# A new order for the opening of an attention-plus-MLP kernel, more staging places for its weight blocks, and more low halves on GpSimd

## The chip, the cores and the metric

One NeuronCore of a Trainium2 chip runs the kernel. The metric is the device time of one execution in microseconds (us). PE is TensorE, DVE is VectorE, ACT is ScalarE, POOL is GpSimd, and SP is the queue that issues most DMAs.

## The reference

```
a    = softmax(phi)                      # b,h,s,m   b=8 h=8 s=576 m=32
k_m, v_m = a^T k, a^T v                  # b,h,m,d   d=64
attn = softmax(q k_m^T / 8)              # b,h,s,m
x    = concat over heads of attn @ v_m   # 4608 tokens x 512
h    = x @ w_in                          # 512 -> 2048
out  = (h - tanh(h)) @ w_out             # 2048 -> 512
```

Inputs are float32, the weights come as 64-bit floats, and the output is 4608 x 512 float32.

## The kernel before

The weights are not applied to x. Per batch b the kernel folds v_m into w_in: P(b, fb) = v_m @ w_in for each of four blocks fb of 512 hidden columns. A unit u is 256 tokens (18 units, and some lie across two batches), so h(u, fb) = attn @ P(b, fb). A polynomial for h - tanh(h) follows, and then the product with w_out. To get nearly float32 accuracy out of 16-bit matmuls, each factor is split into a high and a low half (f16), and three products of halves are summed.

The work is written by hand as a list of words, and at the end every engine's instructions are pinned to the order in which they were written (`in_order`). So each engine, and each DMA queue, is a strict queue: an instruction that waits holds up all that stand behind it. The list `START` is the opening. It covers units 0 to 3 and the first two blocks of unit 4; after it a loop (steady part) runs the same steps for the other 54 blocks by a plan. The words:

- `iK:tag` and `oK:tag` load one 512 KB block K of w_in or w_out (as 64-bit words) into a buffer of the ring `tag`; with the tags `kv2` and `kv3` two blocks. In the profile these are the tiles `raw` and `raws` (L373, L380). A ring with n buffers can take a new load only when the (n)th load before it has been consumed; until then SP waits, and all later loads with it.
- `FX` and `FA` load phi in two layouts (tiles `pt` and `e`), `KA` and `KB` load k and v (tile `kv`, and `kt`), and `Q` loads q for one half t of a batch (tile `q`, L139).
- `Tpp` converts a pair p of weight blocks to float32 on DVE (L386, L391, L396, two instructions each, into `wt`, by way of the ring in `W_TAG`) and casts the high half on ACT (L408). Its low half is made by `Lp` (PE and ACT), by `Lv` (DVE, L421, two instructions) or by `L` (a scaling on ACT, L437, and a subtraction on POOL, L440, two each). Pairs 0 to 7 are w_in (two pairs for one fb), 8 to 15 w_out.
- `X`, `YX`, `XT`, `V`, `N`, `U`, `UV`: softmax of phi, k_m and v_m, the transpose to `kT`, `vh` and `vl`. `S` forms scores (psc, L278); `AM`, `AE`, `AD`, `AT`, `AS` are the softmax over them and its split into `ah` and `al`. `AM` and `AD` subtract and multiply on POOL (L308, L321), and `AS` makes `al` on POOL, `ASv` on DVE (both L522).
- `P` and `PL` (or `PLp`) make the halves of P. `Hufb` is the first matmul (L579). The words `a` and `ap` run the polynomial: DVE L594, ACT L599, DVE L604, ACT L610 (the high half of g). With `ap` the first DVE step leaves its result in PSUM; with `a` it goes to one of two `h3` buffers in SBUF. The low half of g is made by `c` on POOL or by `cv` on DVE (both L615). `Mufb` is the second matmul (24 matmuls, L658); its last eight need the low half.
- `Z` is two matmuls of no use to the result, which fill gaps on PE (tile `warm`, L798). `G`, `R`, `OP`, `O` prepare the steady part and store results.

Of the kernel before, what the change touches and what calls it, by code (L numbers as in the profile page):

```python
# [63 lines left out]
START = """
i0:gg i1:gg T00 T00 Z00 Z00 FX0 T00 X0 T00 YX0 Z00 Z00 Z00 Z00 Z00 Z00 Z00 Z00 Z00 Z00 i6:kv3 T03 i4:kv2 T03 i2:gg Z00
T02 T03 i3:gg T02 T02 Z00 KA0 Z00 Z00 Z00 KB0 Lp00 Lp00 o2:gg o3:gg Q00 T01 T03 XT0 Lp03 XT0 V00 Z00 Z00 T01 T01 T02
Q01 T01 o4:gg Lv01 o5:pp2 V01 N0 Z00 U0 L02 U0 Z00 S00 Z00 S01 T09 T09 T09 S00 o6:gg KA1 L02 KB1 AM00 S01 AM00 Lp03 UV0
UV0 o7:gg AM01 W0 T09 AM01 AE00 AE01 AD00 AD01 AD00 AT00 AD01 Z00 Z00 Z00 P00 AT01 FX1 P00 Lp09 PLp00 Z00 ASv00 P01
PLp00 ASv00 T10 Lp09 P01 AS01 H00 H00 T10 T11 PL01 i10:kv3 o9:pp4 X1 Q10 ap00 Q11 o1:gg AS01 T10 o0:pp2 T11 YX1 ap00
H10 XT1 T11 ap00 H10 XT1 T10 Lv10 ap00 c00 V10 V11 T11 L11 H11 N1 a10 U1 T08 i8:kv2 T08 UV1 U1 S10 UV1 T08 KA2 a10 T08  # L70
H11 a10 S10 H01 Lv08 a10 c10 S11 M00 ap11 AM10 W1 P10 H01 o10:pp5 o8:gg ap11 S11 ap11 M10 AM10 AE10 AM11 KB2 FA2 P10
Q20 AD10 L11 AM11 ap01 PL10 Q21 P11 T12 T12 ap01 AE11 ap11 AD10 T12 cv11 T12 P11 M11 AT10 AD11 AS10 AS10 ap01 H20 PL11
AD11 Lv12 AT11 T05 T05 ap01 T05 H21 OP1 cv01 H20 FX2 T05 ap20 H21 AS11 ap20 o11:gg AS11 X2 ap20 M01 a21 H31 L05 OP0 T04
T04 T04 a21 ap20 cv20 XP2 a21 H31 ap31 Y2 T04 L05 i14:kv3 L04 a21 L04 H30 c21 H30 a30 T13 M20 Y2 P02 i12:kv2 M21 T13
ap31 a30 P02 T13 V20 V21 a30 PL02 ap31 H02 H12 T06 T06 T06 T13 L13 OP2 T06 P12 a30 Lv06 ap31 T07 T07 N2 T07 cv30 T07 W2
M30 Lv07 P12 o12:kv2 cv31 H02 PL12 a02 P03 H12 P03 a02 T14 T14 T14 PL03 M31 ap12 a02 FA3 T14 OP3 L13 U2 ap12 Lv14 U2
UV2 o14:kv3 UV2 a02 H13 S20 ap12 S20 H13 ap12 H03 c02 AM20 a13 H03 T15 a03 P13 M02 P13 a13 S21 PL13 c12 AM20 H22 T15
a03 H23 a13 AE20 a13 G00 c13 S21 P20 AMv21 H22 AD20 a22 T15 T15 AD20 a03 a03 a22 G01 Lv15 AT20 P20 H23 a22 AMv21 AE21
cv03 ap23 R1 a22 ASv20 PL20 M12 ap23 M13 P21 ap23 FQ3 H32 ap23 P21 H32 ASv20 O1 O1 AD21 PL21 a32 H40 H40 G10 ap40 c22
R0 AD21 cv23 G20 AT21 ap40 a32 G11 ap40 H41 M03 H33 P22 AS21 H33 a32 a32 M22 P22 c32 O0 M23 X3 G21 H41 ap41 G30 ap33  # L80
G31 PL22 ap41 O0 ap33 ap40 KR30 R2 P23 P23 O2 ap41 c40 AS21 O2 ap33 ap33 F40 cv33 ap41 M32 M33 R3 O3 O3 PL23 c41
"""
# [261 lines left out]
def split_path(ctx, tc, c, ins, out):  # L344
# [37 lines left out]
    def to_f32(p, ts):  # L382

        r32 = [raws.pop(2 * p + i).bitcast(U32).rearrange("p (f w) -> p f w", w=2) for i in range(2)]
        for r, t in zip(r32, ts):
            nc.vector.tensor_scalar(  # L386
                t, r[:, :, 1], 3, 0x3FFFFFFF, op0=ALU.logical_shift_left, op1=ALU.bitwise_and
            )
        yield
        for r, t in zip(r32, ts):  # L390
            nc.vector.scalar_tensor_tensor(  # L391
                t, r[:, :, 0], 29, t, op0=ALU.logical_shift_right, op1=ALU.bitwise_or
            )
# [708 lines left out]
@with_exitstack  # L1102
def tile_kernel(ctx: ExitStack, tc: tile.TileContext, qt, kva, kvt, pha, phx, w_in, w_out, out):
    nc = tc.nc
    ins = dict(qt=qt, kva=kva, kvt=kvt, pha=pha, phx=phx, w_in=w_in, w_out=w_out)
# [8 lines left out]
    nc.vector.tensor_scalar(c["nid16"], c["ident"], -1.0, None, op0=ALU.mult)
# [50 lines left out]
```

## Time and profile before

| | |
|---|---|
| median of 3 runs | 655.64 us (655.16 to 656.02) |
| profiled execution, its own time | 652.95 us |
| span of the profiled execution | 651.2 us |
| mean granted TensorE clock | 0.999 |
| PE busy | 631.0 us, 97% |
| DVE busy | 525.5 us, 81% |
| ACT busy | 375.0 us, 58% |
| POOL busy | 250.8 us, 39% |
| end of the opening (first matmul of tile `hs`) | 191.91 us |

The time of an execution is 1.75 us more than its span, and the profiled one was 2.69 us below the median of the timed runs. The profile's rows are in us from the span's start; a step of an engine begins when the step before it on that engine has begun to drain, so the distance between two starts is some 0.08 us shorter than a duration on DVE, and for matmuls much shorter.

### The profile page before, as it was taken

The numbers are of one execution on the slowest core, as the hardware profiler recorded it, in microseconds if no ns is written. First come the engines' busy times: TensorE is split into PE (matmuls) and PEld (weight loads), VectorE is DVE, ScalarE is ACT, GpSimd is POOL, SyncE is SP. The second block draws the span as 40 slices with busy tenths as digits, with TensorE's granted clock in tenths as the row PEclk, the third lists the DMA queues.
The fourth block names the chain that finished last, engine by engine and source line by source line (L and its number), as shares of the span: only waits on it lengthen the run. The fifth ranks groups of instructions, "written<-read, shape, count | busy, mean of one in ns | idle before, by whom it ended". The sixth has DMA issues, their size and how long they took to land.

```text
span 651.2 us, 15451 instructions
## 1 busy us (share of the span) xinstructions
PE 631.0 (97%) x6618; PEld 451.7 (69%) x6618; DVE 525.5 (81%) x786; ACT 375.0 (58%) x505; POOL 250.8 (39%) x173
## 2 busy tenths in 40 slices
PE   8679999999999999999999999999999999999996
PEld 4255656566557768777777777777787777887885
DVE  6889999999956687877888879787979786867773
ACT  4477686666524456544655565545655677666541
POOL 0225141222132254452536353635452455455531
PEclk9999999999999999999999999999999999999999
DMA  8999344301422302145313522441354333234201
GB/s 342 390 381 372 109 179 168 119 15 67 147 97 104 135 33 73 37 153 171 104 49 143 170 65 75 155 145 60 106 156 135 102 115 113 67 113 133 79 33 38
DMA packets 27724, 85.51 MB, mean 131 GB/s; under 512 B 3584, under 2 KB 4096, under 8 KB 26880
## 3 DMA queue, kind: packets, MB, share of 16 engines
q1 hardware_dynamic: 26352, 82.08, 36.8%
q10 hardware_dynamic: 1296, 2.36, 1.0%
q8 instruction: 54, 0.88, 0.6%
q14 instruction: 22, 0.18, 0.1%
HBM read 72.89 MB, written 11.54 MB: 130 GB/s over the span
## 4 chain that ended last, share of the span: by engine, by line
PE 68%; DVE 21%; ACT 4%; issue 3%; DMA 2%; POOL 1%; DVEq 0%; ACTq 0%; POOLq 0%
PE hs L579 17%; PE x L722 12%; PE o L715 11%; PE o L722 8%; PE o L658 6%; DVE f L628 4%; PE h L579 4%; PE o1h L658 3%; DVE h L604 3%; DVE h L594 3%; DMA raw<-in_w_out_dram 2%; PE pp L531 2%; DVE ph L549 2%; DVE wt L391 1%; PE warm L798 1%
## 5 line engine op out<-in xcount | busy, mean ns | idle before, releaser
L615 POOL TENSOR_TENSOR g<-h,g 128x1024 f16<-128x1024 f32 x64 | 138.0, 2157 | 323.7 <-ACT g L610 223.8
L579 PEld LDWEIGHTS <-ph 128*128 128x128 f16 x2304 | 177.4, 98 | 19.5 <-issue 5.6
L579 PE MATMUL hs<-ah,ph 128*128 128x256 f16 (+3 forms) x1152 | 151.4, 246 | 0.0
L594 DVE SCALAR_TENSOR_TENSOR h<-hs,u 128x1024 f32<-128x1024 f32 x54 | 65.9, 1221 | 81.2 <-ACT u L586 81.2
L610 ACT ACTIVATE g<-h 128x1024 f16<-128x1024 f32 x72 | 76.0, 1057 | 94.5 <-DVE h L604 92.5
L579 PE MATMUL hs<-al,ph 128*128 128x256 f16 (+3 forms) x576 | 127.6, 246 | 0.0
L599 ACT ACTIVATE u<-u,beta 128x1024 f32<-128x1024 f32 x72 | 82.5, 1149 | 55.4 <-DVE h L594 54.4
L715 PE MATMUL o<-wout_hi,g 128*128 128x512 f16 x432 | 104.7, 379 | 0.0
L722 PEld LDWEIGHTS <-f 128*128 128x128 f16 x896 | 87.7, 98 | 10.2
L604 DVE SCALAR_TENSOR_TENSOR h<-u,h 128x1024 f32<-128x1024 f32 x72 | 87.4, 1216 | 0.8 <-ACT u L599 0.7
L722 PE MATMUL x<-bt,f 128*128 128x256 f16 x672 | 82.5, 273 | 0.0
L722 PEld LDWEIGHTS <-g 128*128 128x128 f16 x672 | 64.4, 98 | 25.8 <-issue 3.8
L586 ACT ACTIVATE u<-hs 128x1024 f32<-128x1024 f32 x54 | 55.1, 1020 | 44.4 <-PE hs L579 39.5
L628 DVE TENSOR_TENSOR f<-g 128x512 f16<-128x512 f16 x112 | 68.6, 652 | 4.3 <-POOL g L615 3.4
L715 PEld LDWEIGHTS <-g 128*128 128x128 f16 x432 | 40.6, 98 | 43.8 <-issue 8.0
L658 PEld LDWEIGHTS <-g 128*128 128x128 f16 x384 | 36.7, 98 | 46.5 <-issue 3.4
L658 PE MATMUL o<-wout_hi,g 128*128 128x512 f16 x192 | 58.8, 379 | 0.0
L579 PE MATMUL h<-ah,ph 128*128 128x256 f16 (+3 forms) x384 | 49.6, 246 | 0.4 <-DVE h L604 0.4
L579 PE MATMUL h<-al,ph 128*128 128x256 f16 (+2 forms) x192 | 42.4, 246 | 0.2 <-POOL al L522 0.2
L549 DVE SCALAR_TENSOR_TENSOR ph<-pp,ph 128x1024 f16<-128x1024 f32 x31 | 37.6, 1214 | 1.4 <-ACT ph L544 1.4
L544 ACT ACTIVATE ph<-pp 128x1024 f16<-128x1024 f32 x32 | 32.6, 1018 | 7.5 <-PE pp L531 5.1
L658 PE MATMUL o<-wout_lo,g 128*128 128x512 f16 x96 | 36.4, 379 | 0.0
(145 smaller groups left out, 962.3 us busy)
## 6 DMA issues: line engine op xcount, KB each, us to landing
q<-in_qt_dram SPq DMA_DIRECT2D x16, 576.0 KB, 4.4
...
```

The source lines that it names most:

```text
L549: nc.vector.scalar_tensor_tensor(pl, pa, S_P / (S_V * S_W), ph, op0=ALU.mult, op1=ALU.subtract)
L579: nc.tensor.matmul(hp[:, k, tu : tu + w], px[:, g, cs], d[ax][:, g, ta : ta + w], start=(n == 0), stop=(n == 5),)
L586: nc.scalar.activation(uu, hp, AF.Square, scale=1.0 / (S_A * S_P))
L594: nc.vector.scalar_tensor_tensor(h3, hp, C2 * S_G / (S_A * S_P), uu, op0=ALU.mult, op1=ALU.mult)
L599: nc.scalar.activation(uu, uu, AF.Square, bias=c["beta"])
L604: nc.vector.scalar_tensor_tensor(h3, uu, CC, hp, op0=ALU.add, op1=ALU.mult)
L610: nc.scalar.activation(gg[:, 0], h3, AF.Copy)
L615: eng.tensor_tensor(gg[:, 1], h3, gg[:, 0], op=ALU.subtract)
L628: nc.vector.tensor_tensor(o, x, y, op=op)
L658: nc.tensor.matmul(o, gx[:, k, P * tt : P * tt + P], wx[:, 4 * fb + k, :], start=(first and k == 0 and wx is wout_hi and gx is gh), stop=( ...
L715: nc.tensor.matmul(o[th], gg[:, 0, k, P * th : P * th + P], wout_hi[:, 4 * fb + k, :], start=(first and k == 0), stop=False)
L722: nc.tensor.matmul(dst, a(1 - n, kk), b(n, kk), start=(new and kk == 0 and n == 0), stop=(end and kk == 1 and n == 1))
```

## The change

Three things in one edit. The list `START` is written anew: the same steps in another order, with other rings for the loads. `W_TAG` spreads the float32 weights over four rings instead of two: two new ones, `us` and `qt`, which hold a pair in one place and are otherwise used by the steady part. And other variants of the same step are chosen: of the 16 low halves of weight pairs 10 instead of 5 are made on POOL, 5 instead of 8 on DVE, 1 instead of 3 on PE and ACT; of the 18 low halves of g 16 instead of 10 on POOL; `al` always on POOL; one multiplication `AD` on DVE; and 14 instead of 8 of the 18 polynomials run by `a` instead of `ap`. The steady part is untouched.

```diff
 START = """
-i0:gg i1:gg T00 T00 Z00 Z00 FX0 T00 X0 T00 YX0 Z00 Z00 Z00 Z00 Z00 Z00 Z00 Z00 Z00 Z00 i6:kv3 T03 i4:kv2 T03 i2:gg Z00
...
+Z00 Z00 KB0 Z00 Z00 FX0 i3:pp4 Z00 i2:h3 Z00 Z00 X0 Z00 Z00 KA0 T01 YX0 XT0 T01 i0:sc Z00 i1:pp1 T01 Q00 XT0 V00 V01
...
-W_TAG = ["pr" if p in (1, 3, 9, 11) else "ot" for p in range(16)]
+W_TAG = "pr us us qt qt ot us pr pr ot us us ot qt qt us".split()
...
+    def new_pair(p):
+        if W_TAG[p] in ("us", "qt"):
+            t = big.tile([P, 2, 512], U32, tag=W_TAG[p], name=f"wt{p}", bufs=1)
+            return [t[:, i] for i in range(2)]
+        return [big.tile([P, 512], U32, tag=W_TAG[p], name=f"wt{p}{i}") for i in range(2)]
+
     def conv(p):
 
-        ts = [big.tile([P, 512], U32, tag=W_TAG[p], name=f"wt{p}{i}") for i in range(2)]
+        ts = new_pair(p)
         yield from to_f32(p, ts)
```

Lines behind the new function stand six further down in the changed kernel (L440 becomes L446, L615 becomes L621).

First place: the SP queue up to the loads of q for batch 0. The number behind `raw` is the block (0 to 15 w_in, 16 to 31 w_out), `kv00` and `kv01` are the two halves of k and v. Before, from the eighth load on:

```order
L373 DMA raw2_158<-in_w_in_dram 128x512
L373 DMA raw3_168<-in_w_in_dram 128x512
L113 DMA kv00_176<-in_kva_dram 128x2064
L121 DMA kt0_178<-in_kvt_dram 128x516
L113 DMA kv01_186<-in_kva_dram 128x2064
L373 DMA raw18_194<-in_w_out_dram 128x512
L373 DMA raw19_196<-in_w_out_dram 128x512
L139 DMA q00_198<-in_qt_dram 128x1152
L139 DMA q01_253<-in_qt_dram 128x1152
```

After, from the first load:

```order
L113 DMA kv01_106<-in_kva_dram 128x2064
L104 DMA pt0_112<-in_phx_dram 128x1152
L373 DMA raw3_114<-in_w_in_dram 128x512
L373 DMA raw2_118<-in_w_in_dram 128x512
L113 DMA kv00_130<-in_kva_dram 128x2064
L121 DMA kt0_132<-in_kvt_dram 128x516
L373 DMA raw0_153<-in_w_in_dram 128x512
L373 DMA raw1_157<-in_w_in_dram 128x512
L139 DMA q00_161<-in_qt_dram 128x1152
L139 DMA q01_207<-in_qt_dram 128x1152
```

The two loads of q were the 15th and 16th of the queue, behind ten weight blocks that shared the three buffers of `gg` and the two of each `kv` pair; they are now the 9th and 10th, behind four weight blocks that lie in four different places.

Second place: POOL, from the first low half of g. Before:

```order
L615 TENSOR_TENSOR g00_592<-h300_581,g00_592 128x1024
L615 TENSOR_TENSOR g10_740<-h310_670,g10_740 128x1024
L308 TENSOR_TENSOR sc1_698<-sc1_698,sm10_779 128x576
L440 TENSOR_TENSOR wout_lo_100<-wt110_513,wout_hi_99 128x512
L440 TENSOR_TENSOR wout_lo_100<-wt111_514,wout_hi_99 128x512
L308 TENSOR_TENSOR sc1_698<-sc1_698,sm11_847 128x576
L321 TENSOR_TENSOR sc1_698<-sc1_698,sz10_857 128x576
L522 TENSOR_TENSOR al1_942<-af1_935,ah1_941 128x2x288
L321 TENSOR_TENSOR sc1_698<-sc1_698,sz11_937 128x576
L522 TENSOR_TENSOR al1_942<-af1_935,ah1_941 128x2x288
```

After:

```order
L446 TENSOR_TENSOR wout_lo_100<-wt90_510,wout_hi_99 128x512
L446 TENSOR_TENSOR wout_lo_100<-wt91_511,wout_hi_99 128x512
L446 TENSOR_TENSOR wout_lo_100<-wt80_519,wout_hi_99 128x512
L446 TENSOR_TENSOR wout_lo_100<-wt81_520,wout_hi_99 128x512
L308 TENSOR_TENSOR sc1_682<-sc1_682,sm10_697 128x576
L621 TENSOR_TENSOR g00_695<-h300_515,g00_695 128x1024
L621 TENSOR_TENSOR g10_703<-h310_622,g10_703 128x1024
L321 TENSOR_TENSOR sc1_682<-sc1_682,sz10_739 128x576
L446 TENSOR_TENSOR wout_lo_100<-wt10_700,wout_hi_99 128x512 x2
L308 TENSOR_TENSOR sc1_682<-sc1_682,sm11_808 128x576
L528 TENSOR_TENSOR al1_838<-af1_835,ah1_837 128x2x288
L621 TENSOR_TENSOR g11_806<-h311_737,g11_806 128x1024
```

Four low halves of w_out now stand ahead of the first low half of g on this queue, and the low halves of g(1,1) and later blocks have come onto it.

Third place: DVE around `dg2`, for which PE waits with the first matmul of batch 2 (tile `pmx`). Before:

```order
L396 SCALAR_TENSOR_TENSOR wt51_1002<-raws10_518,wt51_1002 128x512
L615 TENSOR_TENSOR g01_1007<-h301_945,g01_1007 128x1024
L594 SCALAR_TENSOR_TENSOR h20_947<-h20_947,u20_1069 128x1024
L151 TENSOR_REDUCE mx2_1083<-pt2_1071 128x2
L157 TENSOR_TENSOR dg2_1085<-ident_58,mx2_1083 128x256
L604 SCALAR_TENSOR_TENSOR h320_1087<-u20_1069,h20_947 128x1024
```

After:

```order
L391 SCALAR_TENSOR_TENSOR wt4_1013<-raws8_565,wt4_1013 128x512 x2
L610 SCALAR_TENSOR_TENSOR h320_949<-u20_941,h320_949 128x1024
L396 SCALAR_TENSOR_TENSOR wt4_1013<-raws8_565,wt4_1013 128x512 x2
L151 TENSOR_REDUCE mx2_1084<-pt2_883 128x2
L157 TENSOR_TENSOR dg2_1086<-ident_58,mx2_1084 128x256
L386 TENSOR_SCALAR wt70_1100<-raws14_1016 128x512
```

The low half of g(0,1) has gone from this queue to POOL, and the whole conversion of pair 4 and the second polynomial step of g(2,0) now stand ahead of `dg2`.

More of the change, by code (lines that the diff above doesn't have):

```diff
@@ L64 @@
 START = """
-i0:gg i1:gg T00 T00 Z00 Z00 FX0 T00 X0 T00 YX0 Z00 Z00 Z00 Z00 Z00 Z00 Z00 Z00 Z00 Z00 i6:kv3 T03 i4:kv2 T03 i2:gg Z00
[L66 to L79, printed above, removed]
@@ L80 @@
-R0 AD21 cv23 G20 AT21 ap40 a32 G11 ap40 H41 M03 H33 P22 AS21 H33 a32 a32 M22 P22 c32 O0 M23 X3 G21 H41 ap41 G30 ap33
-G31 PL22 ap41 O0 ap33 ap40 KR30 R2 P23 P23 O2 ap41 c40 AS21 O2 ap33 ap33 F40 cv33 ap41 M32 M33 R3 O3 O3 PL23 c41
+Z00 Z00 KB0 Z00 Z00 FX0 i3:pp4 Z00 i2:h3 Z00 Z00 X0 Z00 Z00 KA0 T01 YX0 XT0 T01 i0:sc Z00 i1:pp1 T01 Q00 XT0 V00 V01
+Q01 i6:kv3 N0 T00 Z00 T01 o1:gg i4:kv2 W0 U0 Z00 L01 U0 T00 o3:q UV0 Z00 L01 T00 S00 S00 AM00 S01 UV0 S01 o2:pp2 AM00
+Z00 Z00 T00 AM01 Lp00 AE00 T03 Z00 AD00 AM01 Z00 Lp00 P00 T03 Z00 AE01 o0:pp3 P00 Z00 AD01 Z00 AD00 AT00 T03 AS00 AD01
@@ new lines @@
+AT01 Z00 FX1 PLp00 T02 KB1 KA1 T03 PLp00 L03 T02 Z00 AS01 Z00 AS00 T02 T02 Lv02 L03 AS01 H00 X1 Z00 P01 H00 P01 YX1
+Q10 H10 T09 PL01 a00 H10 T08 XT1 XT1 T09 H11 i8:kv2 o5:sc T09 V10 V11 Z00 a00 o4:pp2 T08 T09 a10 L09 N1 T08 U1 a10 T08
+Q11 H01 L09 U1 UV1 S10 a00 o6:pp5 L08 UV1 a10 H11 L08 S10 a00 AM10 AM10 T10 a10 Z00 AE10 H01 o7:pp4 T10 FA2 T10 S11
+i10:kv3 c00 c10 S11 o9:pp5 T10 a11 AD10 M00 a01 AD10 a11 P10 a11 L10 P10 L10 a01 a11 AM11 M10 AT10 AS10 AM11 W1 PL10
+AS10 T11 AE11 P11 T11 c11 T11 T11 FX2 a01 P11 Lv11 a01 H20 H20 AD11 AD11 AT11 a20 AS11 M11 PL11 a20 T05 T05 c01 M01
@@ new lines @@
+KB2 T05 T04 i14:kv3 OP1 T04 a20 T04 H21 AS11 T05 X2 OP0 L05 a20 T07 i12:kv2 H30 XP2 Y2 T04 H21 c20 M20 L04 H30 a21
+o10:sc T07 a21 a21 T06 L04 KA2 L05 P02 a21 Y2 o8:q H31 o11:gg c21 T07 T06 T06 P02 T07 ap30 ap30 H31 PL02 ap30 M21 T13
+a31 V20 ap30 a31 V21 T13 N2 H02 P12 L07 T12 H12 c30 L07 T06 OP2 P12 o12:kv2 a31 Q21 H02 Lv06 PL12 ap02 a31 H12 c31 a12
+T12 T12 T13 ap02 M30 o14:kv3 ap02 T15 P03 M31 FA3 U2 P03 T15 T13 PL03 Q20 ap02 T12 c02 UV2 U2 Lv13 H03 T14 UV2 S20 W2
+a12 L12 S20 OP3 H13 P13 a12 T14 a12 P13 T14 L12 AMv20 H13 AMv20 a13 H03 a13 a03 T14 a13 M02 H22 a03 PL13 a03 FQ3 a13
@@ L82 @@
+S21 T15 S21 H22 AE20 a22 a22 a03 AM21 ADv20 H23 G00 P20 cv03 c12 c13 P20 M12 P21 ADv20 PL20 H23 T15 H32 a23 AM21 a22
+L15 Lv14 AE21 a23 G20 P21 R1 L15 AT20 AS20 X3 M13 O1 PL21 H32 M03 a23 a22 P22 H33 c22 AD21 O1 a32 AS20 H33 G21 R0 a32
+P22 O0 a23 AD21 G10 O0 AT21 H40 M22 c23 PL22 a33 a32 P23 M23 H40 a32 AS21 a33 G01 ap40 c32 a33 G30 R2 a33 ap40 O2 ap40
+H41 O2 KR30 M32 ap40 c40 H41 ap41 cv33 F40 G11 G31 M33 R3 ap41 AS21 P23 PL23 ap41 O3 O3 ap41 c41
 """
-W_TAG = ["pr" if p in (1, 3, 9, 11) else "ot" for p in range(16)]
+W_TAG = "pr us us qt qt ot us pr pr ot us us ot qt qt us".split()
```

## The prediction

> **What bounds the kernel now.** I read the page first, for which engine is busy in which stretch. Its 40 slices are 16.3 us each:
>
> ```profile
> PE   8679999999999999999999999999999999999996
> DVE  6889999999956687877888879787979786867773
> POOL 0225141222132254452536353635452455455531
> GB/s 342 390 381 372 109 179 168 119 15 67 147 97 104 135 33 73 37 153 171 104 49 143 170 65 75 155 145 60 106 156 135 102 115 113 67 113 133 79 33 38
> ```
>
> PE is full from the fifth slice on. In the first four the DMAs run at their full rate (near 390 GB/s) and DVE is close to full until the tenth. So the change, which touches the opening alone, can act on PE only early. I then cut the span at the places where PE passes marks that both kernels have, and asked for each stretch's busy time (columns: length; busy us of PE, PEld, DVE, ACT, POOL with their instructions; clock; DMA share; GB/s):
>
> ```profile
> 0.00:37.00 37.00, 28.66 (x271) 12.37 (x271) 27.56 (x55) 18.71 (x31) 7.86 (x16) 1.00 0.95 368
> 37.00:58.10 21.10, 16.63 (x231) 12.77 (x224) 19.96 (x32) 16.31 (x27) 3.75 (x3) 1.00 1.00 379
> 58.10:88.50 30.40, 30.40 (x267) 17.40 (x265) 29.91 (x44) 20.05 (x28) 13.62 (x11) 1.00 0.56 204
> 88.50:191.90 103.40, 102.93 (x958) 59.41 (x957) 93.88 (x120) 61.50 (x77) 26.46 (x16) 1.00 0.31 104
> 191.90:651.20 459.30, 452.36 (x4907) 349.73 (x4905) 354.14 (x538) 258.44 (x345) 199.07 (x128) 1.00 0.31 102
> ```
>
> PE is idle for 8.34 us before 37.0 us (the first `H`), for 4.47 us from there to 58.1 us (the first `M`), and after it for 0.47 us in 133.8 us of the opening. The marks are these rows of the order of time and, the second, of the chain that ended last (start, length):
>
> ```profile
> 36.99 0.28 PE L579 MATMUL h<-ah,ph 128*128 128x256 f16 x1
> ...
> 58.12 5.29 PE o L658 x24
> ...
> 88.52 0.60 PE L170 MATMUL pmx<-dg,ones 128*128 128x256 f32 x2
> ...
> 191.91 0.22 PE L579 MATMUL hs<-ah,ph 128*128 128x128 f16 x1
> ```
>
> PE's work after the first `M` is the same words in both kernels, nearly in the same order. It follows that the end moves by what the first `M` moves, less what PE newly waits for behind it. The sum is made of these two.
>
> **Why the first H starts at 37 us.** The queue of loads (SP) shows it:
>
> ```profile
> 4.35 4.05 SPq L373 DMA_DIRECT2D raw<-in_w_in_dram  x2
> ...
> 10.25 9.52 SPq L373 DMA_DIRECT2D raw<-in_w_out_dram  x2
> 19.82 0.90 SPq L139 DMA_DIRECT2D q<-in_qt_dram  x2
> ...
> 36.04 0.33 SPq L104 DMA_DIRECT2D pt<-in_phx_dram  x1
> ```
>
> Between the two weight loads at 10.25 us lie 9.5 us in which SP waits for a buffer of `gg`; both loads of q stand behind. From the second half of k and v (21.06), through `kT` and q, to the first `H` the rows are
>
> ```profile
> 4.56 0.43 DVE L386 TENSOR_SCALAR wt<-raw 128x512 uint32<-128x512 uint32 x1 [2.71 <-DMA raw<-in_w_in_dram]
> ...
> 21.06 1.09 PE L238 MATMUL pkv<-kv,e 128*32 128x129 f32 x32 [1.02 <-DMA kv<-in_kva_dram]
> ...
> 24.05 0.28 ACT L270 ACTIVATE kT<-ptr 128x128 f32<-128x128 f32 x1 [2.32 <-PE ptr L266]
> ...
> 26.24 0.72 PE L278 MATMUL psc<-q,kT 64*32 64x288 f32 x16 [1.80 <-DMA q<-in_qt_dram]
> 27.46 0.77 DVE L287 STREAM_TRANSPOSE sc<-psc 128x576 f32<-128x576 f32 x1
> ...
> 34.57 0.69 ACT L520 ACTIVATE ah<-af 128x576 f16<-128x576 f32 x1 [1.17 <-DVE af L326]
> ...
> 35.94 0.72 DVE L522 TENSOR_TENSOR al<-af,ah 128x576 f16<-128x576 f32 x1
> ```
>
> `kT` is ready 3.3 us after PE began on the second half of k and v, q comes 1.8 us later still, and from the scores to the first `H` it takes 10.75 us.
>
> **Step 1, the loads: scores 7.9 us earlier.** The first 0.524 MB block is down at 4.56 us (the first L386 starts there). In the new order q00 is down after kv01, pt, four blocks, kv00, kt and itself, 5.66 MB: 5.13 MB more at 390 GB/s are 13.2 us, so 17.7 us, and q01 at 19.2 us. Nothing ahead waits for a buffer: the four blocks lie in four places. The scores also need `kT`: kv00 is down at 12.9 us by the same rate, its half takes 1.1 us on PE, the other half to `kT` 3.3 us as before, and ACT now has two scalings (`L01`, 1.1 us) ahead of `kT`: near 18.3 us. So the scores start at 18.35 instead of 26.24 us.
>
> **Step 2, from scores to first H: 1.4 us longer.** The conversion of pair 3 now stands on DVE between the softmax steps of batch 0 (two L386 of 0.43, and four L391 and L396 of 0.68 us, priced below), which delays the second transpose by some 1.5 us; `al` costs 1.28 us on POOL instead of 0.72 on DVE, where it waited 0.68 us behind the other half. Last comes the low half of P, behind two casts on ACT. I get 12.15 us instead of 10.75, and the first `H` at 30.5 us (6.5 earlier).
>
> **Step 3, from first H to first M: 20.5 instead of 21.1 us.** Three `Z` and one `P` (0.6 us) move behind the first `H`: 16.63 + 1.9 = 18.5 us of PE work, so 49.0 us at the earliest. The first `M` needs the high half of g(0,0), and its queue sets 51 us:
>
> ```profile
> 47.43 1.21 DVE L604 SCALAR_TENSOR_TENSOR h<-u,h 128x1024 f32<-128x1024 f32 x1
> ...
> 48.67 1.06 ACT L610 ACTIVATE g<-h 128x1024 f16<-128x1024 f32 x1 [0.31 <-DVE h L604]
> ```
>
> In the new order DVE has one pair of weights less ahead of that L604 (2 x 0.43 + 4 x 0.68 = 3.6 us) and no `al` (0.7), but one L594 (1.2) and one `N` (0.8) more: 2.3 us less, so it ends at 46.3 us, and at 47.8 us with the late blocks of step 2. ACT then has two casts, `kT`, `vh`, two scalings and one square ahead of the high half (3.1 us), and the low half of w_out block 0 comes off POOL at about the same time. So the first `M` is at 51.0 us, 7.05 us earlier, with 49 and 53 as its bounds.
>
> **Step 4, what the moved low halves cost and save.** The prices (group: count, busy, mean ns) in the opening:
>
> ```profile
> L615 DVE TENSOR_TENSOR g<-h,g 128x1024 f16<-128x1024 f32 x8 | 9.7, 1217 | 0.0
> L615 POOL TENSOR_TENSOR g<-h,g 128x1024 f16<-128x1024 f32 x10 | 21.6, 2166 | 78.7 <-ACT g L610 78.7
> L391 DVE SCALAR_TENSOR_TENSOR wt<-raws,wt 128x512 uint32<-128x512 uint32 x16 | 10.3, 684 | 0.0
> L421 DVE SCALAR_TENSOR_TENSOR wout_lo<-wt,wout_hi 128x512 f16<-128x512 f32 x10 | 6.4, 679 | 0.0
> L440 POOL TENSOR_TENSOR wout_lo<-wt,wout_hi 128x512 f16<-128x512 f32 x4 | 4.6, 1161 | 4.3 <-ACT wt L437 4.3
> L437 ACT ACTIVATE wt<-wt 128x512 f32<-128x512 f32 x10 | 5.7, 618 | 0.0
> ```
>
> DVE loses six L615 (7.3 us), six L421 (4.1) and two L522 (1.5), and gains one multiplication (0.7): 12.2 us less. POOL gains six L615 (13.0), ten L440 (11.6) and two L522 (2.6) and loses one L321 (1.2): 26 us more on the 52 that the four stretches show. ACT gains ten L437 (6.2) and loses two copies of an L610's shape (2.1): 4.1 us more on 117, hidden by its idle time but for step 3's. PE loses two `Lp` before the first `H`, where it waits anyway: nothing. A low half that comes 1 us later costs PE nothing, since only the last 8 of the 24 matmuls of an `M` read it, two thirds of 5.29 us, 3.5 us, after the start. Six more `a` instead of `ap` change no instruction's count.
>
> What could hold PE behind the first `M` is DVE. The place is `dg2`, the third place shown:
>
> ```profile
> 83.29 0.87 DVE L157 TENSOR_TENSOR dg<-ident,mx 128x256 f32<-128x256 f32 x1
> ```
>
> It ends at 84.2 us, 4.4 us before PE takes it. Ahead of it DVE has four L421 (2.7 us), two L615 (2.4) and one L522 (0.7) fewer and one L604 (1.2) more: 4.6 us less, so 79.5 us plus what more POOL work costs DVE. PE comes there at 88.52 - 7.05 = 81.5 us. POOL has 27 instead of 17 tensor instructions ahead of it, 14.75 us more. What one of them costs DVE is not one number:
>
> ```profile
> 126.27 4.23 POOL L615 TENSOR_TENSOR g<-h,g 128x1024 f16<-128x1024 f32 x2 [23.57 <-ACT g L610]
> ...
> 129.58 2.50 DVE L386 TENSOR_SCALAR wt<-raws 128x512 uint32<-128x512 uint32 x2
> ...
> 84.15 2.28 POOL L440 TENSOR_TENSOR win_lo<-wt,win_hi 128x512 f16<-128x512 f32 x2 [0.28 <-ACT wt L437]
> ...
> 84.08 1.21 DVE L604 SCALAR_TENSOR_TENSOR h<-u,h 128x1024 f32<-128x1024 f32 x1
> ```
>
> Beside the 4.23 us of L615 two L386 took 2.50 us instead of about 0.8: 1.7 us lost, 0.4 per us of POOL. Beside the 2.28 us of L440 an L604 and the L594 behind it lost nothing. The bounds are 0 and 0.4 x 14.75 = 5.9 us. Of the 14.75 us, 7.0 are L440, which is nearest to the second pair of rows and costs nothing, and 7.8 are L615 and L522, nearest to the first: 0.4 x 7.8 = 3 us, which I take. `dg2` is then ready at 82.5 us and PE waits 1.0 us. After it the saving on DVE grows from 4.6 to 12.2 us, so I cost nothing there.
>
> The Trainium skill (SBUF — State Buffer, "Who interferes with whom") says that GpSimd and VectorE share one pair of ports under an exclusive lock, which a VectorE instruction takes if it runs in a two-port mode or has two inputs in SBUF. The stretched L386 agree, and so does the L604 at 84.08 us, whose second input lay in PSUM. By that rule the conversions (L386, L391, L396), L421 and L604 of the `a` kind are what POOL can stop, and this speaks against a change that adds POOL work and moves `ap` to `a`; its price is a rival below.
>
> **The sum.** First `M` -7.05, wait at `dg2` +1.0: -6.0 us. The profiled execution of 652.95 us would become 646.9; against the median of 655.64, which it was 2.69 us below, I predict 649.6 us. With a first `M` at 49 and no cost on DVE, -9.0: 646.6. With 5.9 us on DVE, `dg2` comes at 85.4 us, 3.1 us before 88.52: 652.5, and the same with a first `M` at 53 besides.
>
> **The rivals.**
>
> *The lock takes it all, no change.* Ahead of `dg2` stand 20 L386, 40 L391 and L396, four L421 and five L604, 44 us of work, of 68 in all (DVE's 77.4 us of the first three stretches, less the last 4.3 and the 4.6 saved): POOL would meet such work two times in three. If each meeting stops DVE for POOL's whole time, 14.75 x 2/3 = 9.8 us, `dg2` is ready at 89.3 us, PE loses 0.8 us: 656.4. For it: the stretched L386. Against it: it can as well be POOL's instruction that waits, and POOL has room. 1 in 10.
>
> *Slower, by the same place.* If POOL's queue also runs late, since now two `h3` buffers wait for POOL's low halves before DVE may write the next polynomial step, DVE loses all 14.75 us: `dg2` at 94.3 us, 5.8 us late: 661.4. It decides from 9.0 us of new loss on (79.5 + 9.0 = 88.5). Against it: POOL has 52 us of work in 192, and sat idle 78.7 us before its L615. 1 in 10, with others of its sign 13 in 100.
>
> *The PE clock falls in the opening.*
>
> ```profile
> 1.70 8.88 PE L798 MATMUL warm<-nid 128*128 128x512 f16 x34 [1.70 <-DVE nid L1114]
> ...
> 8.55 1.35 DVE L204 TENSOR_REDUCE mx<-pt 128x2 f32<-128x1152 f32 x1
> ...
> 9.94 1.45 ACT L209 ACTIVATE pt<-pt,mx 128x576 f32<-128x576 f32 x2 [0.63 <-DVE mx L204]
> ```
>
> Before, 34 of these (17 `Z`) kept PE busy to 10.6 us; now 18 do, to about 7.0 us. pt is down at 7.4 us (1.65 MB), its maximum and exponentials take 2.9 us as before, and PE idles 3.3 us until 10.3. If the clock halves, `XT`, `V`, `U` and the scores (5 us) take twice as long and the scores come at 22 to 23 us: 653.6. The Trainium skill (TensorE: Matmul & The Clock Gate, "What's actually happening") puts the window of idleness that halves the clock at about 3.4 us; no trace here has a gap that long. 7 in 100.
>
> *More than forecast*, below 646.5: 5 in 100.
>
> **Chances.** Forecast 65 in 100 (646.5 to 653.5). 0.2%, 1.3 us, is about what a measurement of this kernel can tell from no change. Faster: forecast, clock, more: 77 in 100. Within 0.2%: 10. Slower: 13. The range reaches from 646.5 to 656.5: up to the lock's no change, and what lies beyond on either side is 18 in 100.
>
> **What would show it.** The first wait of PE for q near 18 us and no long wait on SP before it; the first L579 near 30.5 us, the first L658 near 51, `pmx` near 82.5, `hs` near 186; DVE busy some 12 us less and POOL 26 us more before `hs`. I am wrong if the first L658 is later than 55 us, or if PE has idle time behind it beyond 2 us.

## The result, and the profile after

The change makes the kernel slower. After: 678.92 us, median of four runs (676.49 to 679.83); before, on the same chip: 655.4 us (655.0 to 656.02). The ratio is 1.0352 [1.0323, 1.0381]. The forecast was 649.6 us, with a range from 646.5 to 656.5. The profiled execution of the changed kernel took 676.49 us, its span is 674.1.

The page of the changed kernel, its engines:

```profile
PE 634.9 (94%) x6606; PEld 451.7 (67%) x6606; DVE 542.4 (80%) x773; ACT 377.2 (56%) x513; POOL 284.6 (42%) x190
```

DVE has fewer instructions than before (773 for 786), but is busy longer (542.4 for 525.5 us). The same stretches as in the prediction, cut at the marks of the changed kernel (first `H`, first `M`, end of `dg2`, first `hs`; columns as there):

```profile
0.00:32.20 32.20, 23.99 (x229) 10.32 (x230) 21.74 (x37) 12.52 (x23) 9.54 (x17) 0.95 0.83 325
32.20:57.70 25.50, 21.25 (x253) 14.20 (x252) 25.27 (x35) 19.49 (x30) 10.35 (x8) 0.93 0.83 311
57.70:97.90 40.20, 33.11 (x272) 17.66 (x264) 38.69 (x47) 21.26 (x33) 20.40 (x13) 0.96 0.36 123
97.90:214.00 116.10, 104.16 (x956) 59.77 (x957) 100.72 (x118) 64.86 (x84) 43.19 (x25) 1.00 0.36 129
214.00:674.10 460.10, 452.40 (x4907) 349.74 (x4905) 355.97 (x541) 259.10 (x346) 201.11 (x129) 1.00 0.32 103
```

The steady part is as long as before (460.1 against 459.3 us). Nearly all of the loss is in the opening, which ends at 214.0 instead of 191.9 us: 22.1 us. The first `M` comes 0.4 us earlier than before; the way from there to `pmx` takes 9.8 us more (40.2 against 30.4) and the way from `pmx` to `hs` 12.7 us more (116.1 against 103.4). In the opening PE is idle for 31.5 us (214.0 less its 182.5 busy) against 13.3 before, 18.2 more; and its busy time grew by 3.9 us, which goes with the clock column of the first three stretches (0.93 to 0.96). DVE's four stretches sum to 186.4 us against 171.3. That is 15.1 us more, although by the prediction's count its steps should take 12.2 us less: some 27 us have been lost inside DVE's instructions. Between its instructions DVE sat idle for 27.6 us, 7.0 more than before; only 3.2 us of its waits are for POOL's work of the opening (1.9 for a low half of g, 1.3 for a product of the softmax).

Where the 27 us were lost stands in the groups of DVE up to the end of the opening (count, busy, mean ns). Before, the four groups of L391 and L396 had means of 683, 684, 683 and 695 ns:

```profile
L391 DVE SCALAR_TENSOR_TENSOR wt<-raw,wt 128x512 uint32<-128x512 uint32 x16 | 18.5, 1192 | 0.0
L396 DVE SCALAR_TENSOR_TENSOR wt<-raws,wt 128x512 uint32<-128x512 uint32 x16 | 17.7, 1148 | 0.0
L391 DVE SCALAR_TENSOR_TENSOR wt<-raws,wt 128x512 uint32<-128x512 uint32 x16 | 13.1, 858 | 0.0
L396 DVE SCALAR_TENSOR_TENSOR wt<-raw,wt 128x512 uint32<-128x512 uint32 x16 | 12.3, 813 | 0.0
```

The four groups of conversions alone hold 20 us more (61.6 against 41.4). One place in the order of time shows how, and what PE pays:

```profile
59.58 4.84 POOL L621 TENSOR_TENSOR g<-h,g 128x1024 f16<-128x1024 f32 x2
59.82 5.14 DVE L391 SCALAR_TENSOR_TENSOR wt<-raw,wt 128x512 uint32<-128x512 uint32 x2
64.89 1.28 DVE L396 SCALAR_TENSOR_TENSOR wt<-raw,wt 128x512 uint32<-128x512 uint32 x2
66.09 0.77 DVE L287 STREAM_TRANSPOSE sc<-psc 128x576 f32<-128x576 f32 x1
66.92 0.63 PE L537 MATMUL pp<-win_hi,vh 64*32 64x512 f16 x8 [3.08 <-DVE sc L287]
```

Two L391 beside two low halves of g on POOL take 5.14 us; the two L396 behind them, with POOL idle, 1.28 us. PE needs the transpose L287, which stands behind them on DVE, and waits 3.08 us. Then it runs at half clock for a while (the clock is the third number from the end):

```profile
67.00:70.00 3.00, 3.00 (x28) 0.83 (x28) 2.93 (x5) 1.99 (x3) 0.72 (x1) 0.50 0.00 0
```

### The profile page after: what moved, and what is told of

The parts are those of the page before. It is cut to its first block, busy times and chain, and to the rows that moved or that the text cites. A ratio compares the mean times of both kernels' runs of the same rounds, so it can differ in the third digit from the quotient of the medians.

```text
span 674.1 us, 15412 instructions
## 1 busy us (share of the span) xinstructions
PE 634.9 (94%) x6606; PEld 451.7 (67%) x6606; DVE 542.4 (80%) x773; ACT 377.2 (56%) x513; POOL 284.6 (42%) x190
## 4 chain that ended last, share of the span: by engine, by line
PE 57%; DVE 28%; ACT 5%; issue 4%; DMA 3%; POOL 1%; SPq 0%; ACTq 0%; DVEq 0%; POOLq 0%
PE hs L585 16%; PE x L728 11%; PE o L721 10%; PE o L728 8%; DVE f L634 4%; DVE h L600 4%; DVE h L610 4%; DVE wt L391 3%; PE h L585 3%; DVE wt L396 3%; PE o L664 2%; DVE ph L555 2%; PE pp L537 2%; DMA d<-ot 2%; ACT u L592 2%
## 5 line engine op out<-in xcount | busy, mean ns | idle before, releaser
L621 POOL TENSOR_TENSOR g<-h,g 128x1024 f16<-128x1024 f32 x70 | 152.8, 2183 | 311.0 <-ACT g L616 207.0
L600 DVE SCALAR_TENSOR_TENSOR h<-hs,u 128x1024 f32<-128x1024 f32 x54 | 66.0, 1221 | 80.4 <-ACT u L592 80.3
L610 DVE SCALAR_TENSOR_TENSOR h<-u,h 128x1024 f32<-128x1024 f32 x72 | 89.7, 1245 | 2.3 <-ACT u L605 2.2
L585 PE MATMUL h<-ah,ph 128*128 128x256 f16 (+3 forms) x384 | 52.0, 250 | 3.5 <-ACT ph L564 1.9
```

Of the source, the lines that this page charges most:

```text
L585: nc.tensor.matmul(hp[:, k, tu : tu + w], px[:, g, cs], d[ax][:, g, ta : ta + w], start=(n == 0), stop=(n == 5),)
L600: nc.vector.scalar_tensor_tensor(h3, hp, C2 * S_G / (S_A * S_P), uu, op0=ALU.mult, op1=ALU.mult)
L610: nc.vector.scalar_tensor_tensor(h3, uu, CC, hp, op0=ALU.add, op1=ALU.mult)
L621: eng.tensor_tensor(gg[:, 1], h3, gg[:, 0], op=ALU.subtract)
```

## The experiments

Three theories stood against each other: POOL's instructions stop DVE's (called the lock in the first four expectations); the new order itself makes engines wait for each other; a longer queue on POOL holds up what stands in it. Each ratio is to the kernel before, run on the same chip.

### e1 to e4: giving the work back, and moving it alone

e1, e2 and e4 edit the new list; e3 edits the old one. In e1 the pairs 3 and 9, which were on PE and ACT before, went to DVE.

```diff
 # e1: every step of the new order on its engine of before
-L01 L01  L03 L03  Lv02  c11  c01  AS00  ADv20  AMv20 ...
+Lv01     Lv03     L02 L02  cv11 cv01 ASv00 AD20 AM20 ...
 # e2: ten weight pairs of the new order
-L01 L01  (and 3, 4, 5, 7, 8, 9, 10, 12, 15)
+Lv01     (and 3, 4, 5, 7, 8, 9, 10, 12, 15)
 # e3: the old order
-Lv01 Lp09 Lv08 Lv10 Lv12 Lv15  cv11 cv01 cv20 cv23  ASv00 ASv20
+L01  L09  L08  L10  L12  L15   c11  c01  c20  c23   AS00  AS20
 # e4: six low halves of g of the new order
-c11  c01  c20  c30  c31  c23
+cv11 cv01 cv20 cv30 cv31 cv23
```

> The changed order, rings and loads, but every low half, multiplication and subtraction on the engine that made it before (POOL has 28 tensor instructions in the opening again, as before, instead of 42; DVE gets back 12 us of work). Lock theory (POOL's new work and DVE's two-input work stop each other, which the trace after shows as L391 of up to 2.6 us): the stretches go, and most of the 23 us come back: 653 to 662 us. Order theory (the new order itself makes DVE and PE wait at the wrong places, and who makes a low half matters little): 12 us more DVE work in the same order, so no better than after: 676 to 690 us.

> The changed kernel with the ten low halves of weight pairs that POOL makes (20 subtractions, 27 us on POOL in the trace after) moved to DVE (20 more L427 of 0.68 us, 13.6 us), 20 scalings on ACT left out; the low halves of g stay on POOL. Lock theory: most of the long L391 and L396 stand beside these 20 subtractions or beside the low halves of g in equal parts, so about half of the 29 us of stretch goes and 13.6 come on: 672 to 682 us, about as after, with the stretch per conversion near half. Order theory: 13.6 us more on DVE with nothing back: 685 to 695 us.

> The kernel before, order, rings and loads untouched, with six low halves of weight pairs (1, 8, 9, 10, 12, 15), four low halves of g ((0,1), (1,1), (2,0), (2,3)) and both al that DVE or PE made moved to POOL: some 25 us more POOL work and 13 us less DVE work in the opening, nearly the change's own shift. Lock theory: DVE loses more than it saves: 660 to 675 us, with L391 and L396 stretched beyond 1.2 us in the rows. Order theory: DVE has less to do in an order that works: 650 to 656 us.

> The changed kernel with six of its sixteen low halves of g on POOL (those that DVE made before: (0,1), (1,1), (2,0), (2,3), (3,0), (3,1)) moved back to DVE: POOL loses 13 us, DVE gains 7.3. Lock theory: the stretches beside these six go (each up to 1.9 us on one or two conversions): 668 to 677 us. Order theory: 7 us more on DVE: 680 to 688 us.

Measured: e1 682.75 us, 1.0437 [1.041, 1.0463]; e2 683.35, 1.0446 [1.042, 1.0473]; e4 680.69, 1.0409 [1.0376, 1.0441]; e3 666.92, 1.0191 [1.0164, 1.0218]. e1 and e4 lie in the ranges of the order theory, e2 between the two, e3 in that of the lock. So in the old order the move costs 12.7 us (e11 and e12 below show that not all of it is the lock's); but in the new order giving the work back brings nothing, and in e1 and e2 costs more. As the only cause, the moved work fell. The groups of e1 show why that does not clear POOL:

```profile
L391 DVE SCALAR_TENSOR_TENSOR wt<-raw,wt 128x512 uint32<-128x512 uint32 x16 | 13.2, 866 | 0.0
L391 DVE SCALAR_TENSOR_TENSOR wt<-raws,wt 128x512 uint32<-128x512 uint32 x16 | 13.1, 862 | 0.0
L396 DVE SCALAR_TENSOR_TENSOR wt<-raws,wt 128x512 uint32<-128x512 uint32 x16 | 12.8, 841 | 0.0
L396 DVE SCALAR_TENSOR_TENSOR wt<-raw,wt 128x512 uint32<-128x512 uint32 x16 | 12.1, 804 | 0.0
```

POOL's work up to the end of the opening is near that of before here (55.3 against 51.7 us), yet the conversions take 51.2 us instead of 41.4. In the old order none of the 32 L391 ran beside a POOL instruction, in e1 seven did. The new order exposes POOL work that the old one had kept beside other steps.

### e8: the price by itself

```diff
+    for dve, n, pool, m in (
+        (merge, 8, low_w, 0), (shift, 0, low_w, 6), (shift, 0, low_g, 6), (merge, 12, low_w, 10), (shift, 12, low_w, 10),
+        (merge, 12, low_g, 8), (shift, 12, low_g, 8), (cubic_sb, 10, low_g, 8), (cubic_ps, 10, low_g, 8), (cubic_ps, 10, low_w, 10),
+    ):
...
+        meet()
```

Each entry is a stage: n steps of DVE beside m steps of POOL, and `meet` has DVE wait for both before the next stage.

> The disputed cost by itself; everything else of the kernel is left out and the output is filled with a constant. Stages one after the other: DVE's merge of a weight block (as L391, two SBUF inputs, 128x512) alone; POOL's low half of a weight (as L446, 128x512) alone; POOL's low half of g (as L621, 128x1024) alone; then merge beside L446, the shift (as L386, one SBUF input) beside L446, merge beside L621, shift beside L621, then the 128x1024 step of the polynomial with two SBUF inputs beside L621, and the one with a PSUM and an SBUF input beside L621 and beside L446. Theory 1: merges and shifts beside POOL take turns with it one for one, so a merge takes about 0.6 + 1.1 = 1.7 us beside L446 and 0.6 + 2.1 = 2.7 us beside L621, POOL's own steps grow by 0.6 us, and the step with a PSUM input stays at its 1.13 to 1.22 us. Theory 2, no turns: a merge beside POOL stays under 1 us, and the long ones in the trace come from something else that only the full kernel has.

It was run once. DVE in the order of time (L53 merge, L50 shift, L59 two SBUF inputs, L56 a PSUM and an SBUF input), and in the second fence POOL's second kind alone, and beside L56:

```profile
7.05 5.71 DVE L53 SCALAR_TENSOR_TENSOR wt<-raw,wt 128x512 uint32<-128x512 uint32 x8
...
33.71 16.99 DVE L53 SCALAR_TENSOR_TENSOR wt<-raw,wt 128x512 uint32<-128x512 uint32 x12
50.73 13.81 DVE L50 TENSOR_SCALAR wt<-raw 128x512 uint32<-128x512 uint32 x12
64.58 23.09 DVE L53 SCALAR_TENSOR_TENSOR wt<-raw,wt 128x512 uint32<-128x512 uint32 x12
87.70 19.89 DVE L50 TENSOR_SCALAR wt<-raw 128x512 uint32<-128x512 uint32 x12
107.70 26.96 DVE L59 SCALAR_TENSOR_TENSOR h<-uu,tf 128x1024 f32<-128x1024 f32 x10
134.96 12.55 DVE L56 SCALAR_TENSOR_TENSOR h<-hp,uu 128x1024 f32<-128x1024 f32 x10
```

```profile
20.49 13.11 POOL L65 TENSOR_TENSOR lo<-tf,hi 128x1024 f16<-128x1024 f32 x6 [0.28 <-DVE lo L68]
...
135.00 17.55 POOL L65 TENSOR_TENSOR lo<-tf,hi 128x1024 f16<-128x1024 f32 x8 [2.69 <-DVE lo L68]
```

Alone, a merge comes every 0.72 us. Twelve would take 8.7; beside ten low halves of a weight they took 16.99: DVE lost 0.83 us for each instruction of POOL. Beside eight low halves of g it lost (23.09 - 8.7) / 8 = 1.80 us for each. The shift, with one SBUF input, lost the same (a step every 0.46 us when POOL is done: 0.83 and 1.80), and the step with two SBUF inputs some 1.85 (ten would take 12.2 at the 1.22 us that such a step takes alone in the full kernel). The step with a PSUM input lost nothing: ten took 12.55 us beside either kind of POOL's work, 1.22 us each, as in the full kernel (L600, mean 1206 ns), and POOL's own beat beside it (17.55 us for eight) is the one that it has alone. The two queues take turns, one instruction each, so a short instruction of DVE pays for a long one of POOL every time: a merge beside the low halves comes every 1.56 or 2.53 us, where theory 1 had 1.7 and 2.7.

Which steps are stopped does not go by their length. Nor is it the number of SBUF inputs alone: the shift and L56 have one each, and only the shift is stopped. e8 leaves out the reductions; the changed kernel has them beside POOL, in the steady part:

```profile
340.19 0.74 DVE L317 TENSOR_REDUCE sz<-sc 128x18 f32<-128x576 f32 x1
340.43 2.13 POOL L621 TENSOR_TENSOR g<-h,g 128x1024 f16<-128x1024 f32 x1 [4.13 <-issue]
340.96 1.63 DVE L318 TENSOR_SCALAR sz<-sz 128x18 f32<-128x18 f32 x1
```

The reduction, with its one input in SBUF, took 0.74 us as it does apart from POOL; the tiny L318 behind it, which takes 0.18 us alone, ended only when POOL's low half did.

### e5, e6 and e10: POOL's low halves cut to stubs

```diff
+LOW = 64
...
+    nc.vector.memset(win_lo.rearrange("p a b -> p (a b)").bitcast(F32), 0.0)
+    nc.gpsimd.memset(wout_lo.rearrange("p a b -> p (a b)").bitcast(F32), 0.0)
...
-            nc.gpsimd.tensor_tensor(lo[:, i], tfs[p][i], his[p][:, i], op=ALU.subtract)
+            nc.gpsimd.tensor_tensor(lo[:, i, 0:LOW], tfs[p][i][:, 0:LOW], his[p][:, i, 0:LOW], op=ALU.subtract)
...
+        n = UT
+        if u < 4 and eng is nc.gpsimd:
+            n = LOW // 4
+            short.add((u, fb))
+        eng.tensor_tensor(gg[:, 1, :, 0:n], h3[:, :, 0:n], gg[:, 0, :, 0:n], op=ALU.subtract)
...
+        gh, gl = gg[:, 0], gg[:, 0 if (u, fb) in short else 1]
```

e5 is this in the new list, e6 in the old one; e10 has the last line alone (and the `short` that it asks), with POOL's work whole. So all three leave low halves, or a part of them, out of the result.

> The changed kernel with the POOL work that the change added (and its like) cut to a stub: the subtractions for the low halves of weights (L446 in the change) and for the low halves of g of units 0 to 3 (L621, by the word c) cover one eighth and one sixteenth of their columns. The rest of the low weights is zero (one memset on DVE and one on POOL before the first load has landed), and M reads the high half of such a g in place of its low half, so it waits for ACT alone. Theory 1, DVE pays for POOL: in the change DVE loses 32.3 us up to the last M33 in steps drawn out beside POOL work, against 3.6 us in the kernel before; with the stubs the lost time falls to some 5 to 10 us, and the kernel, with the same order and loads, to 645 to 657 us. Theory 2, the order alone: DVE's waits (29.9 us) and the late loads stay, a stub on POOL gives back no more than a quarter of the 24 us lost, and it takes 670 to 680 us. Between, the two share it.

> The kernel before with the same stubs for low halves on POOL (10 subtractions of weights and 8 of g), the same memsets, and M reading the high half where the low one is a stub. Both theories: DVE loses only 3.6 us beside POOL here, so it takes 649 to 655 us, within 5 us of the unchanged kernel. Were POOL's work as dear in this order as in the new one, it would fall below 645 us.

> The changed kernel with POOL's work whole, but M of units 0 to 3 reads the high half of g in place of a low half that POOL makes, so it doesn't wait for POOL. e5 did that too, and this run takes it apart from the stubs. Theory 1: POOL still draws out DVE's steps, M's wait for POOL was not the price, and it takes 674 to 680 us. Theory 2: the price was that M waited for low halves on a longer queue of POOL; then it falls to 660 to 668 us.

Measured: e5 660.16 us, 1.0086 [1.0062, 1.011]; e6 656.34, 1.0028 [1.0012, 1.0044]; e10 678.45, 1.0372 [1.0346, 1.0398]. The changed kernel lost 23.5 us to the kernel before, e5 loses 5.0: the stubs take off 18.5. They take nothing off the old order (e6 loses 1.2), where the first `M` comes 3.5 us later with the memsets. M's wait for POOL's low halves is not the price: without it (e10, in the range of its theory 1) the ratio is that of the whole change within its interval. e5 ended 3 us above its range and e6 1.3 us above its own; next to e6, with the same stubs and memsets, 3.8 us of the loss are left. The conversions of e5 (its lines are L394 and L399):

```profile
L399 DVE SCALAR_TENSOR_TENSOR wt<-raws,wt 128x512 uint32<-128x512 uint32 x16 | 12.4, 816 | 0.0
L394 DVE SCALAR_TENSOR_TENSOR wt<-raw,wt 128x512 uint32<-128x512 uint32 x16 | 11.4, 750 | 0.0
L394 DVE SCALAR_TENSOR_TENSOR wt<-raws,wt 128x512 uint32<-128x512 uint32 x16 | 11.3, 747 | 0.0
L399 DVE SCALAR_TENSOR_TENSOR wt<-raw,wt 128x512 uint32<-128x512 uint32 x16 | 10.5, 704 | 0.0
```

They take 45.6 us instead of the 61.6 of the changed kernel: DVE gets back 16.0 us in these four groups, not far from the 18.5 us that the kernel gets back.

### e9: the order without POOL's low halves

e1 with the edit of e5, so part of the low halves is left out here too.

> e1 (the new order, loads and rings with every step on the engine that it had before) with the stubs of e5: 10 subtractions of weights and 8 low halves of g on POOL cut to an eighth and a sixteenth of their columns, the rest of the low weights zero, M reading the high half of such a g. e1 took 682.75 us, with 17.2 us of DVE's steps drawn out and 37.7 us of DVE waiting up to the last M33, against 3.6 and 21.0 us before. Theory 1, POOL's work beside DVE is the cost of the new order too (drawn-out steps, and then others that wait for DVE): 655 to 666 us. Theory 2, the order makes DVE wait whatever POOL does: DVE's waits stay over 30 us and it takes 670 to 680 us.

Measured: 669.89 us, 1.0247 [1.0218, 1.0276], between the two theories: e1 lost 28.5 us to the kernel before and e9 loses 15.8, so the stubs take off 12.7, and 14.7 us over e6 stay. The stretch from 58 to 190 us, as it stands in the kernel before, the changed one, e1, e9 and e5, one row of each:

```profile
58.00:190.00 132.00, 131.53 (x1220) 76.02 (x1213) 123.68 (x163) 81.65 (x104) 39.93 (x27) 1.00 0.37 127
```

```profile
58.00:190.00 132.00, 112.97 (x1054) 65.15 (x1053) 121.22 (x145) 74.55 (x105) 54.67 (x34) 0.99 0.36 128
```

```profile
58.00:190.00 132.00, 111.94 (x972) 61.23 (x972) 116.39 (x150) 70.45 (x98) 37.75 (x24) 0.95 0.34 121
```

```profile
58.00:190.00 132.00, 123.81 (x1125) 69.59 (x1126) 118.76 (x162) 75.31 (x103) 18.71 (x24) 0.96 0.35 127
```

```profile
58.00:190.00 132.00, 124.95 (x1175) 72.47 (x1174) 113.89 (x153) 83.14 (x113) 22.93 (x36) 1.00 0.39 136
```

PE's matmuls in this window: 1220, 1054, 972, 1125, 1175. With the stubs e9 gets back most of what e1 lost, but PE still idles 8.2 us in it and runs at a mean clock of 0.96. So the new order also loses without POOL's low halves; in the changed kernel the steps taken off DVE make up for most of that (e5 loses some 11 us less than e9). Not all of it is the order's own: up to the end of the opening DVE is busy for 183.4 us in e9 and 176.3 in e6, and of these 7.1 us the low halves of pairs 3 and 9 explain 2.7; most of the rest are conversions and other steps still drawn out beside the work that POOL has left (the conversions take 43.9 us against 41.2). How much the order costs by waits alone, and which words do it, stays open.

### e7: q earlier in the old order

```diff
-KB0 Lp00 Lp00 o2:gg o3:gg Q00 T01 ... T02 Q01 T01
+KB0 Q00 Q01 Lp00 Lp00 o2:gg o3:gg T01 ... T02 T01
```

> The kernel before with the two loads of q for batch 0 moved up behind k and v, ahead of the two w_out blocks o2 and o3; nothing else. It is the first step of the prediction alone: q was waited for, and the first scores start at 26.24 us. If that wait is worth its length, the scores start some 3 to 6 us earlier and the kernel takes 650 to 653 us; if DVE's conversions or the later w_out blocks end last there, the scores come earlier and the time stays within 1 us of 654 to 655 us.

Measured: 655.64 us, 1.0017 [1.0005, 1.0028]: no gain. The first scores start at 24.87 us, 1.4 us earlier. But the w_out blocks, now behind q, come later, and DVE converts them ahead of the scores' transposes (L288 here):

```profile
26.54 0.43 DVE L387 TENSOR_SCALAR wt<-raw 128x512 uint32<-128x512 uint32 x1 [2.59 <-DMA raw<-in_w_out_dram]
...
30.57 0.78 DVE L288 STREAM_TRANSPOSE sc<-psc 128x576 f32<-128x576 f32 x1
```

The transpose starts at 30.57 instead of 27.46 us. The wait for q was removed, and a wait for the next load took its place, on an engine that is a strict queue.

### e11 and e12: the two halves of e3 apart

e11 has the six weight pairs of e3's edit alone, e12 the four `c` alone.

> The kernel before with the low halves of six weight pairs (1, 8, 9, 10, 12, 15) moved to POOL, and nothing else: the weights' part of e3, which lost 12.7 us. By e8 a subtraction on POOL beside a conversion costs DVE 0.83 us, and DVE gets back 0.62 us for each of the ten that it no longer makes, so with every one beside a conversion DVE loses about 3.8 us net, with none it gains 6.2 us; PE is busy from 58 us on and would not show the gain. Theory 1 (turns): 655 to 661 us. Theory 2 (the longer POOL queue holds up the low halves of g and the softmax behind it): DVE's and PE's waits grow, and it takes over 662 us.

> The kernel before with the low halves of four blocks of g ((1,1), (0,1), (2,0), (2,3)) moved from DVE to POOL, and nothing else: the other part of e3. DVE saves 4 times 1.13 us; by e8 one such step of POOL costs DVE 1.8 us beside conversions or steps with two SBUF inputs and nothing beside steps with a PSUM input. Theory 1 (turns): between 4.5 us less and 2.7 us more of DVE's time, and 652 to 658 us. Theory 2 (M waits for POOL, whose low half takes 2.16 us in place of 1.13 and stands in a queue): 658 to 664 us.

Measured: e11 661.55 us, 1.011 [1.0088, 1.0132]; e12 663.49, 1.0138 [1.0116, 1.016]. e11 lies between the two ranges, 0.6 us above what turns would give. Together the two lose 16.9 us, more than the 12.7 of e3, so the parts don't add up. e12 is where the theory of the longer queue has it, and its waits from 86 to 107 us show the queue:

```profile
DVE wt L387 <- POOL win_lo L441: 5.6, 1, 5.6
POOL g L616 <- ACT g L611: 4.8, 1, 4.8
...
PE pp L532 <- DVE e L182: 3.8, 1, 3.8
```

A low half of g, which now stands on POOL, waits there 4.8 us for ACT. The low half of a weight pair stands behind it, DVE needs the place of that pair (5.6 us), and PE then waits 3.8 us and halves its clock:

```profile
106.00:108.00 2.00, 1.97 (x26) 0.66 (x27) 2.00 (x3) 2.00 (x2) 1.62 (x1) 0.50 0.17 70
```

So a step moved to POOL has a second price, which no price per instruction contains. How e12's 9.4 us divide is not shown: DVE's steps are drawn out too (busy 174.5 us up to the end of its opening against 171.3 before, with 4.5 us less to do). No run beat the kernel before: its PE is idle for 0.47 us behind the first `M`, so DVE time saved there has nothing to give.

## Why the prediction was wrong, step by step

**Step 1, scores at 18.35 us: right.** They start at 18.04.

```profile
18.04 1.31 PE L278 MATMUL psc<-q,kT 64*32 64x288 f32 x32 [0.66 <-ACT kT L270]
...
32.20 0.27 PE L585 MATMUL h<-ah,ph 128*128 128x256 f16 x1
33.29 0.27 PE L585 MATMUL h<-al,ph 128*128 128x256 f16 x1 [0.83 <-POOL al L528]
35.42 0.39 PE L585 MATMUL h<-ah,ph 128*128 128x256 f16 x2 [1.86 <-ACT ph L564]
```

**Step 2, first H at 30.5 us: it failed on the price of its conversions.** They were costed at 0.68 us each. Two L396 of pair 1, ahead of the first transpose of the scores, took 3.21 us beside the low half of a weight on POOL; then, in pair 3, one L391 took 1.64 us and two L396 2.97:

```profile
17.81 3.21 DVE L396 SCALAR_TENSOR_TENSOR wt<-raw,wt 128x512 uint32<-128x512 uint32 x2
...
27.44 1.64 DVE L391 SCALAR_TENSOR_TENSOR wt<-raws,wt 128x512 uint32<-128x512 uint32 x1
...
30.82 2.97 DVE L396 SCALAR_TENSOR_TENSOR wt<-raws,wt 128x512 uint32<-128x512 uint32 x2
```

The first `H` starts at 32.20 and stops twice, for `al` on POOL and for the low half of P, so its work goes on only from 35.42 us.

**Step 3, first M at 51.0 us: it failed.** It came at 57.70, so the 7.05 us that it was to come earlier shrank to 0.4. The wrong term is again DVE's queue ahead of that `M`, undisturbed in the sum; the clock, which stood at 0.93 from 32.2 to 57.7 us, is the other. With the stubs (e5) the first `M` is at 57.18 us, but there the memsets hold up DVE's first steps: in e6 they moved it from 58.1 to 61.6 us. If they cost e5 the same 3.5 us, it would be near 53.7 without them, so by this estimate some 4 of the 6.7 us missed are POOL's. The prediction set 55 us as the mark from which it would be wrong.

**Step 4, the moved low halves: the count was right, their price on DVE was the failed term.** The kernel has 13 DVE instructions fewer and 17 of POOL more, as counted. The price was read from two L386 beside L615 (0.4 us for each us of POOL) and set to nothing for L440, because an L604 beside it lost nothing. e8 shows 0.83 us for each L440 of 1.15 us and 1.80 for each L615 of 2.12, twice that rate, beside conversions and steps with two SBUF inputs; and the DVE neighbour chosen for L440 had an input in PSUM, the kind that POOL does not stop. The rows of the prediction give the higher rate themselves, if they are read by the clock time. The two L386 start at 129.58 us, so only the last 0.9 us of the 4.23 us of L615 (to 130.50) lie beside them, and behind it POOL has another step:

```profile
130.46 1.34 POOL L308 TENSOR_TENSOR sc<-sc,sm 128x576 f32<-128x576 f32 x1
```

The 1.7 us were lost beside some 2.2 us of POOL's work, 0.8 us for each, and not beside 4.23. The three DVE steps beside the rest of L615 (L287, L306, L594) were of the kinds that are not stopped.

There is a second fault in the same term. The price was charged to the 14.75 us of POOL work that is added ahead of `dg2`, never to the POOL work that was already there. The new order moves conversions beside that too. The new loss ahead of `dg2`, taken as 3 us with 5.9 as its bound, became 97.9 - 79.5 = 18.4 us, more than the dearest rival allowed. Nearly all of it is DVE's busy time, 85.7 us up to there against the 68.5 that the prediction had (77.4 less 4.3 and 4.6):

```profile
97.51 0.42 DVE L157 TENSOR_TENSOR dg<-ident,mx 128x256 f32<-128x256 f32 x1
```

**Behind `dg2`, costed at nothing: the largest part of the miss.** The prediction charged no wait of PE there, since DVE would have 12.2 us less to do. From `pmx` to `hs` PE took 12.7 us more than before. It sat idle for 11.9 us there (116.1 less 104.2 busy) instead of 0.5, and its two longest waits, like most of the others, are for DVE:

```profile
PE pp L537 <- DVE kvn L254: 2.5, 1, 2.5
...
PE pp L537 <- DVE e L181: 1.7, 1, 1.7
```

The step L254 stood on DVE behind two L391 that took 3.68 us (from 120.99 us) beside low halves on POOL. So the three parts of the miss are 6.6 us up to the first `M`, 8.8 from there to `pmx` (9.8 more instead of 1.0), and 12.7 behind it. The saving of 12.2 us was real as a count, but the drawn-out steps took it and more.

**The rivals.** The slower one, by `dg2`, had the right sign, at 13 in 100, and its condition, over 9.0 us of new loss ahead of `dg2`, was met twice over; but its 661.4 us stop there, and the waits for `h3` buffers that it named were 1.9 us in the whole opening. The sentence that spoke against it, that POOL has room, was no reason: POOL is busy for 83.5 us of the 214 and DVE is drawn out all the same. The rule of the Trainium skill (SBUF — State Buffer, "Who interferes with whom"), that port sharing is an exclusive lock, was the better guide, and the turns of e8 agree with it; the two meetings in three that the no-change rival counted were an average over steps which the order of words decides one by one. The clock rival was priced at one place, before the scores. It did happen, elsewhere: PE's busy time in the opening grew by 3.9 us. In the changed kernel a wait of 2.44 us, for a step that stood on DVE behind the two L396 of 3.21 us, is followed by a half clock:

```profile
22.75 2.07 PE L435 MATMUL pw<-wt,idw 128*128 128x512 f32 x2 [2.44 <-DVE vl L511]
...
22.60:24.00 1.40, 1.25 (x2) 0.65 (x3) 1.37 (x3) 0.17 (x1) 1.16 (x1) 0.50 1.03 421
```

The window of about 3.4 us that the prediction quoted from the Trainium skill (TensorE: Matmul & The Clock Gate, "What's actually happening") is longer than this wait; the measurement decides. Nor does the length of one wait decide alone: after one of 2.49 us, at 125.46 us, the clock stayed at 1.00.
